# Transposing unscaled probabilities in TensorE's transposing mode, with the row sums applied behind the values

## The chip, the cores and the metric

One core of one Trainium2 chip runs the whole kernel. The metric is the device time of one execution in microseconds (us); the kernel before has a median of 924.71 us over three runs. Everything is f32 at the inputs and outputs. The engines are called TensorE (PE, and PEld for its weight loads), VectorE (DVE), ScalarE (ACT), GpSimd (POOL) and SyncE (SP, which issues most of the transfers).

## The reference

An attention with 8 batches, 8 heads, 512 local and 32 global positions of width 64 feeds a two-layer network:

```python
s_g = scale * np.matmul(q_g, k_all.transpose(0, 1, 3, 2))
out_g = np.matmul(sm(s_g), v_all)
s_ll = scale * np.matmul(q_l, k_l.transpose(0, 1, 3, 2))
mask = np.abs(pos[:, None] - pos[None, :]) <= window      # window = 32
s_ll = np.where(mask, s_ll, -1000000000.0)
s_lg = scale * np.matmul(q_l, k_g.transpose(0, 1, 3, 2))
a_l = sm(np.concatenate([s_lg, s_ll], axis=-1))
out_l = np.matmul(a_l, np.concatenate([v_g, v_l], axis=2))
# all heads side by side: x is 4352 x 512
h = x @ w_in                                                # 512 -> 2048
g = np.maximum(h, 0.0) + np.log1p(np.exp(-np.abs(h)))
out = g @ w_out                                             # 2048 -> 512
```

`sm` subtracts the row's maximum, takes the exponential and divides by the row's sum plus 1e-9.

## The kernel before

The kernel works batch by batch. The network's part is the bulk: for each batch, 16 steps `h` and `g` (first and second half of a 512-long contraction into one PSUM bank of 128x512), an activation chain on ACT, VectorE and POOL, and steps `o` that accumulate four output banks. Both use x, the weights and g as pairs of a rounded value (`hi`) and a remainder (`lo`), so each product is three matmuls. The raw f32 weights have to be taken apart into these pairs first, one tile of 128x512 at a time: `W` (ACT), `b`, `B`, `c` or `C` (the `wbits` instruction on VectorE or on ACT, then one on VectorE) and `N` or `n` (the pair on ACT and POOL, or on ACT and VectorE). All 32 tiles are done in the opening.

The attention of batches 1 to 7 works on transposed scores (`s_ps`, `v_ps`, `mt`, `zt`, `rb`). The first batch has a path of its own, in ten steps: eight local ones (four pairs of heads `m`, halves `a` of two 128-query chunks each) and two global ones. Each has seven stages, written `U<step><stage>`:

- 0, `scores0`: the mask and the scores of 4 x 128 queries by 224 keys in PSUM (`s`), the maxima and the exponentials (`e`, in SBUF) with their sums (VectorE, ACT);
- 1, `invert0`: 1/sum on VectorE;
- 2, `diag0`: POOL multiplies the 128x128 identity by 1/sum, once per score block (`diag`, 128x512);
- 3, `turn0`: plain f32 matmuls of `e` with `diag` give the scaled and transposed probabilities (`t`, one PSUM tile of two banks that all steps share);
- 4, `evict0`: two copies to SBUF (`p_..gh`, `p_..gl`; form `F` puts both on ACT);
- 5, `values0`: the product with the values (`o`, in one of the two banks that `h` uses as well);
- 6, `split0`: ACT rounds it to `xh`, VectorE takes the remainder `xl`. For the global steps (`split0g`) ACT copies it to `yg`, which is stored.

All four `xh`, `xl` of the batch must be there before the first `h`.

The order of all this work is written out by hand in three strings: `OPENING` (first batch's attention, the weights, second batch's attention and the first 16 `h`), `STEADY` (each further batch) and `LAST`. Each token issues its instructions, and `keep` and `inorder` hold each engine to that order. Helpers record each matmul at line 166 and the first batch's stages at lines 194 to 333.

Of the kernel before, what the change touches and what calls it, by code (L numbers as in the profile page):

```python
# [83 lines left out]
def moe_over_global_local_attention(  # L84
# [137 lines left out]
    def invert0(name, n):  # L222

        t = st["sums", name]
        keep("dve", nc.vector.tensor_scalar(t[:, 2, 0:n], t[:, 2, 0:n], 1e-9, None, op0=ALU.add))
        keep("dve", nc.vector.reciprocal(t[:, 0, 0:n], t[:, 2, 0:n]))

    def diag0(name, n):

        t = st.pop(("sums", name))  # L230
        d = st["diag", name] = pl.tile([P, 4, P], F32, tag="xa", name=f"diag{name}", bufs=4)
        keep("pool", nc.gpsimd.tensor_tensor(d[:, 0:n], identf.unsqueeze(1).to_broadcast([P, n, P]), t[:, 0, 0:n].unsqueeze(2).to_broadcast([P, n, P]), op=ALU.mult))
# [39 lines left out]
    def values0(m, a):  # L272
        t, vt = st.pop(("p0", m, a)), st["v0", m]
        ps = st["o0", m, a] = ps_h.tile([P, 512], F32, tag="h", name=f"o0_{m}_{a}")[:, 0:256].rearrange("p (c q) -> p c q", c=2)
        for c in range(2):
# [4 lines left out]

    def split0(m, a):
        ps = st.pop(("o0", m, a))
        if a == 0:
# [3 lines left out]
        keep("act", nc.scalar.copy(hi, ps))
        keep("dve", nc.vector.tensor_tensor(lo, ps, hi.bitcast(F32), op=ALU.subtract))
# [38 lines left out]
    def split0g(n):  # L327
        ps = st.pop(("o0g", n))
        y = pl.tile([P, 2, SG], F32, tag="yg", name=f"yg{n}", bufs=1)
        for h in range(2):  # L330
# [1 line left out]
            keep("act", nc.scalar.copy(y[r], ps[r, 0:P].rearrange("p (i h q) -> p i h q", i=2, h=2)[:, :, h]))
# [437 lines left out]
    local = (scores0, lambda m, a: invert0((m, a), 4), lambda m, a: diag0((m, a), 4), turn0, evict0, values0, split0)  # L770
    glob = (scores0g, lambda n: invert0(n, 1), lambda n: diag0(n, 1), turn0g, evict0g, values0g, split0g)
# [79 lines left out]
```

## Time and profile before

| | before |
|---|---|
| median of 3 runs | 924.71 us (923.99 to 926.71) |
| profiled execution | 925.41 us, of which the span of its instructions is 923.6 us |
| PE busy | 913.3 us, 5,242 matmuls |
| VectorE, ACT, POOL busy | 591.3, 503.9, 443.0 us |
| PE, VectorE, ACT, POOL busy between 8 and 60 us | 50.2, 37.1, 43.2, 17.2 us of 52 |
| the same between 60 and 160 us | 100.0, 87.2, 77.3, 77.4 us of 100 |
| granted TensorE clock | 0.999 |

In the rows of the profile, `t<-diag,e` is an instruction that writes tile t from tiles diag and e; `128*128 128x512` is a matmul with weights of 128x128 and an output of 128x512. In a timeline a row starts with its start and its length in us, and ends with the idle time ahead of it and what ended that. In the chain each row is one link: start, length, engine, tile, line. A row of stretches gives, for each engine, the busy us and the instructions, then the granted clock, the share of the transfer engines and GB/s.

### The profile page before, as it was taken

How to read it: one execution, taken by the hardware profiler on the slowest of the kernel's cores; microseconds unless marked ns; L12 is line 12 of the kernel's file. 1: busy time of each engine (PE TensorE's matmuls, PEld its weight loads, DVE VectorE, ACT ScalarE, POOL GpSimd, SP SyncE). 2: the span in 40 equal slices, each digit the busy share in tenths (PEclk: the TensorE clock that was granted, in tenths of full speed). 3: DMA queues.
4: the chain of work that ended last, by engine and by line, in shares of the span. 5: the costliest groups of instructions: out<-in, count | busy, mean ns of one | idle time of the engine just before them, and what ended most of it. 6: DMA issues, size and time to landing. Idle time of an engine off the chain costs nothing.

```text
span 923.6 us, 14326 instructions
## 1 busy us (share of the span) xinstructions
PE 913.3 (99%) x5242; PEld 751.2 (81%) x5242; DVE 591.3 (64%) x1324; ACT 503.9 (55%) x850; POOL 443.0 (48%) x580
## 2 busy tenths in 40 slices
PE   8999999999999999999999999999999999999997
PEld 4888788888888888888888888888888888888896
DVE  4889988477766868477766868477766868211211
ACT  5878777453554626553554636553554636644453
POOL 2358687263644546262644546272744546222221
PEclk9999999999999999999999999999999999999999
DMA  9582501302022030302021020302021010100000
GB/s 346 193 301 98 197 17 65 113 17 85 17 81 66 10 94 18 114 17 86 18 84 64 11 92 19 113 17 86 17 86 62 14 56 6 65 0 1 24 23 23
DMA packets 30694, 65.02 MB, mean 70 GB/s; under 512 B 7328, under 2 KB 7840, under 8 KB 30624
## 3 DMA queue, kind: packets, MB, share of 16 engines
q1 hardware_dynamic: 29888, 63.78, 20.5%
q8 instruction: 41, 0.67, 0.3%
q10 hardware_dynamic: 736, 0.33, 0.2%
q14 instruction: 29, 0.24, 0.1%
HBM read 54.66 MB, written 9.44 MB: 69 GB/s over the span
## 4 chain that ended last, share of the span: by engine, by line
PE 83%; DVE 7%; issue 4%; POOL 3%; ACT 3%; DMA 0%; ACTq 0%; SPq 0%; DVEq 0%; POOLq 0%
PE o L166 36%; PE h L166 33%; PE s_ps L166 6%; PE v_ps L166 4%; DVE zt L412 2%; PE t L166 1%; DVE zr L472 1%; DVE zt L460 1%; PE s L166 1%; POOL s L445 1%; DVE e L680 1%; POOL gl L684 1%; DVE rb L474 1%; ACT s L450 1%; POOL s L446 1%
## 5 line engine op out<-in xcount | busy, mean ns | idle before, releaser
L166 PE MATMUL o<-wo,gh 128*128 128x512 f32 x1088 | 340.0, 394 | 0.0
L166 PE MATMUL h<-xh,wi 128*128 128x512 f32 (+1 forms) x1152 | 339.6, 378 | 0.0
L684 POOL TENSOR_TENSOR gl<-e,gh 128x512 fp32r<-128x512 f32 x136 | 176.4, 1297 | 290.8 <-ACT gh L683 202.4
L680 DVE SCALAR_TENSOR_TENSOR e<-h,e 128x512 f32<-128x512 f32 x136 | 92.6, 681 | 250.1 <-ACT e L679 244.7
L166 PEld LDWEIGHTS h<-xh,wi 128*128 128x128 f32 x1152 | 212.0, 188 | 41.7 <-issue 1.4
L166 PEld LDWEIGHTS o<-wo,gh 128*128 128x128 f32 x1088 | 200.7, 188 | 46.6 <-issue 7.2
L166 PE MATMUL h<-xl,wi 128*128 128x512 f32 (+1 forms) x576 | 217.3, 377 | 0.0
L166 PE MATMUL o<-wo,gl 128*128 128x512 f32 x544 | 211.7, 389 | 0.0
L677 ACT ACTIVATE e<-h 128x512 f32<-128x512 f32 x136 | 80.5, 592 | 212.3 <-PE h L166 207.4
L683 ACT CAST gh<-e 128x512 fp32r<-128x512 f32 x136 | 84.4, 620 | 132.6 <-DVE e L680 132.6
L166 PEld LDWEIGHTS h<-xl,wi 128*128 128x128 f32 x576 | 108.4, 188 | 20.1
L166 PEld LDWEIGHTS o<-wo,gl 128*128 128x128 f32 x544 | 102.1, 188 | 21.6
L679 ACT ACTIVATE e<-e,one 128x512 f32<-128x512 f32 x136 | 98.6, 725 | 4.4
L445 POOL TENSOR_TENSOR s<-s,mb 128x640 f32<-128x640 f32 x56 | 88.0, 1571 | 22.7 <-DVE mb L434 21.7
L678 ACT ACTIVATE e<-e 128x512 f32<-128x512 f32 x136 | 85.9, 632 | 4.3
L450 ACT ACTIVATE s<-s 128x1024 f32<-128x1024 f32 x56 | 58.6, 1058 | 14.7 <-POOL s L446 14.7
L460 DVE TRANSPOSE_TENSOR_REDUCE zt<-s 128x32 f32<-128x1024 f32 x56 | 65.8, 1212 | 0.5 <-ACT s L450 0.5
L166 PEld LDWEIGHTS s_ps<-raw 64*128 64x128 f32 x672 | 49.6, 186 | 10.6 <-issue 9.7
L166 PE MATMUL s_ps<-raw 64*128 64x160 f32 (+1 forms) x672 | 57.3, 315 | 0.0
L446 POOL TENSOR_TENSOR s<-s,mb 128x384 f32<-128x384 f32 x56 | 56.9, 1015 | 0.0
L395 DVE TRANSPOSE_TENSOR_REDUCE mt<-s 128x32 f32<-128x1024 f32 x48 | 56.7, 1219 | 0.0
L166 PE MATMUL v_ps<-s,v 128*64 128x160 f32 (+3 forms) x784 | 53.8, 291 | 1.1 <-DVE e L680 1.1
(154 smaller groups left out, 799.9 us busy)
## 6 DMA issues: line engine op xcount, KB each, us to landing
raw<-in_qk SPq DMA_DIRECT2D x56, 368.0 KB, 3.6
v<-in_v SPq DMA_DIRECT2D x28, 384.0 KB, 3.1
wiraw<-in_w_in SPq DMA_DIRECT2D x16, 512.0 KB, 8.1
woraw<-in_w_out SPq DMA_DIRECT2D x16, 512.0 KB, 7.0
out<-ot SPq DMA_DIRECT2D x32, 256.0 KB, 2.1
v<-in_v SPq DMA_DIRECT2D x4, 512.0 KB, 9.8
raw<-in_qk SPq DMA_DIRECT2D x4, 416.0 KB, 7.2
raw<-in_qk SPq DMA_DIRECT2D x4, 352.0 KB, 4.0
```

Of the source, the lines that this page charges most:

```text
L166: order["pe"] = after(nc.tensor.matmul(*a, **k), "pe").ins
L395: inorder(nc.vector.tensor_reduce(windows(mt, 16 * p, 32, 2, 16), st["s", m, p].rearrange("p h (b k) -> p h b k", k=32), axis=AX.X, op=ALU ...
L445: inorder(engine.tensor_tensor(sw, sw, pairs(mb, QW, 0, 192, 160), op=ALU.subtract))
L446: inorder(engine.tensor_tensor(s[:, :, 160:352], s[:, :, 160:352], mb[:, :, 64:256], op=ALU.subtract))
L450: inorder(nc.scalar.activation(s, s, AF.Exp, scale=0.125))
L460: inorder(nc.vector.tensor_reduce(windows(zt, 16 * p, 32, 2, 16), st["s", m, p].rearrange("p h (b k) -> p h b k", k=32), axis=AX.X, op=ALU ...
L677: inorder(nc.scalar.activation(e, ph, AF.Abs))
L678: inorder(nc.scalar.activation(e, e, AF.Exp, scale=-1.0))
L679: inorder(nc.scalar.activation(e, e, AF.Ln, bias=one))
L680: inorder(nc.vector.scalar_tensor_tensor(e, ph, 0.0, e, op0=ALU.max, op1=ALU.add))
L683: inorder(nc.scalar.copy(gh, e))
L684: inorder(nc.gpsimd.tensor_tensor(gl, e, gh.bitcast(F32), op=ALU.subtract))
```

## The change

Stage 3 transposes `e` itself, in TensorE's transposing mode against the plain identity. 1/sum is applied to the product with the values instead. For that it has to lie along the free axis of the transposed output: in stage 1 POOL spreads it over columns (`wide`, 128x256, in a buffer that `mt` and `zt` use too), and the new stage 2 (`over0`) transposes `wide` into the second half of the values bank, from where ACT copies it to SBUF (`y`). In stage 6 VectorE multiplies values and `y`, ACT rounds the result and POOL takes the remainder (VectorE in the form `G`, used once). The global steps do the same with 128x128, and VectorE multiplies instead of ACT's copies.

```diff
-    "L10 L20 L00 L21 L01 w L11 L02 K L12 w U00 U01 W w w U02 U10 U20 b U03 U21 F04 U11 w L31 "
...
+    "L10 L00 L20 w L01 w L11 L02 l40 L30 w L12 w L21 L31 w w L22 l42 W W K b U00 U10 w "
...
-    def diag0(name, n):
-
-        t = st.pop(("sums", name))
-        d = st["diag", name] = pl.tile([P, 4, P], F32, tag="xa", name=f"diag{name}", bufs=4)
-        keep("pool", nc.gpsimd.tensor_tensor(d[:, 0:n], identf.unsqueeze(1).to_broadcast([P, n, P]), t[:, 0, 0:n].unsqueeze(2).to_broadcast([P, n, P]), op=ALU.mult))
+        w = st["wide", name] = pl.tile([P, rows_of(349 + 40)], F32, tag="mt", name=f"wide{name}", bufs=3)[:, 0:P if n == 1 else 256]
+        if n == 1:
+            keep("pool", nc.gpsimd.tensor_copy(w, t[:, 0, 0:1].to_broadcast([P, P])))
+        else:
+            for c in range(2):
+                src = windows(t[:, 0], c, 2, 2, 1).to_broadcast([P, 2, 64])
+                keep("pool", nc.gpsimd.tensor_copy(w[:, P * c:P * c + P].rearrange("p (h d) -> p h d", h=2), src))
+
+    def values_bank(key, name):
+        if key not in st:
+            st[key] = ps_h.tile([P, 512], F32, tag="h", name=name)
+        return st[key]
+
+    def over0(m, a):
+        r = st.pop(("wide", (m, a)))
+        ps = values_bank(("o0", m, a), f"o0_{m}_{a}")
+        for c in range(2):
+            mm(ps[:, 256 + P * c:256 + P * c + P], lhsT=r[:, P * c:P * c + P], rhs=identf, start=True, stop=True, is_transpose=True, skip_group_check=True)
+        y = st["y0", m, a] = pl.tile([P, 608], F32, tag="xa", name=f"y0_{m}_{a}", bufs=4)
+        keep("act", nc.scalar.copy(y[:, 0:256], ps[:, 256:512]))
...
     def turn0(m, a):
...
-                mm(ps[:n, i // 2, q:q + P], lhsT=e[:, i, o:o + n], rhs=d[:, i], start=True, stop=True, skip_group_check=True)
+                mm(ps[:n, i // 2, q:q + P], lhsT=e[:, i, o:o + n], rhs=identf, start=True, stop=True, is_transpose=True, skip_group_check=True)
...
-    def split0(m, a):
+    def split0(m, a, engine=nc.gpsimd):
...
-        keep("act", nc.scalar.copy(hi, ps))
-        keep("dve", nc.vector.tensor_tensor(lo, ps, hi.bitcast(F32), op=ALU.subtract))
+        y = st.pop(("y0", m, a))[:, 0:256]
+        keep("dve", nc.vector.tensor_tensor(y, ps[:, 0:256], y, op=ALU.mult))
+        keep("act", nc.scalar.copy(hi, y))
+        keep("pool" if engine is nc.gpsimd else "dve", engine.tensor_tensor(lo, y, hi.bitcast(F32), op=ALU.subtract))
```

The new opening has the same steps in another order, with some of them on other engines: `wbits` is on VectorE 31 times and on ACT once (before 23 and 9), `N` stands 27 times and `n` 5 times (before 26 and 6), one subtraction of the maxima (`Q51`) goes from POOL to VectorE, and one `split0` has the form `G`. The strings for the other batches are the same.

Three places of the order follow. TensorE, from the second step's scores (`s_0_1`) on, before (`raw` holds queries and keys):

```order
L166 MATMUL s_0_1_179<-raw_0_1_120 128x224 x4
L166 LDWEIGHTS ident
L166 MATMUL s_1_0_194<-mask_76,ident 128x448
L166 LDWEIGHTS ident
L166 MATMUL s_1_0_194<-mask_76,ident 128x448
L166 MATMUL s_1_0_194<-raw_1_0_112 128x224 x4
L166 MATMUL t_0_0_212<-diag(0, 0)_177,e_0_0_162 128x128
L166 MATMUL t_0_0_212<-diag(0, 0)_177,e_0_0_162 96x128
```

and now:

```order
L166 MATMUL s_0_1_193<-raw_0_1_120 128x224 x4
L166 MATMUL t_0_0_215<-identf,e_0_0_185 128x128
L166 MATMUL t_0_0_215<-identf,e_0_0_185 96x128
L166 MATMUL t_0_0_215<-identf,e_0_0_185 128x128
L166 MATMUL t_0_0_215<-identf,e_0_0_185 96x128
```

The first turn stands ahead of the third step's scores instead of behind them, and needs `e` alone. Further on in the same queue the spread sums of two steps stand behind the turn of step (1,0), ahead of the scores of (2,1):

```order
L166 MATMUL t_1_0_307<-identf,e_1_0_235 128x128
L166 MATMUL t_1_0_307<-identf,e_1_0_235 96x128
L166 MATMUL o_0_1_329<-identf,wide(0, 1)_245 128x128 x2
L166 MATMUL o_0_0_248<-identf,wide(0, 0)_212 128x128 x2
L166 LDWEIGHTS ident
L166 MATMUL s_2_1_343<-mask_76,ident 128x448
```

Step (0,1) takes its values bank here, several steps ahead of its product with the values. On ACT the first steps read before (`L219` are the exponentials, `L622` is `W`):

```order
L219 ACTIVATE e_0_0_162,sums_0_163<-s_0_0_155,sums_0_163 128x224 x4
L622 ACTIVATE wiraw_122<-wiraw_122 128x512
L219 ACTIVATE e_0_1_186,sums_1_187<-s_0_1_179,sums_1_187 128x224 x4
L219 ACTIVATE e_1_0_201,sums_0_202<-s_1_0_194,sums_0_202 128x224 x4
L266 COPY p_0_0gh<-t_0_0_212 128x512
L268 COPY p_0_0gl<-t_0_0_212 96x512
```

and now, where two `W` go ahead of the exponentials and the first copies stand one step earlier:

```order
L649 ACTIVATE wiraw_118<-wiraw_118 128x512
L649 ACTIVATE wiraw_122<-wiraw_122 128x512
L219 ACTIVATE e_0_0_185,sums_0_186<-s_0_0_178,sums_0_186 128x224 x4
L219 ACTIVATE e_0_1_200,sums_1_201<-s_0_1_193,sums_1_201 128x224 x4
L287 COPY p_0_0gh<-t_0_0_215 128x512
L289 COPY p_0_0gl<-t_0_0_215 96x512
```

More of the change, by code (lines that the diff above doesn't have):

```diff
@@ L226, in invert0, with over0g @@
         keep("dve", nc.vector.reciprocal(t[:, 0, 0:n], t[:, 2, 0:n]))
-    def diag0(name, n):
-        t = st.pop(("sums", name))
-        d = st["diag", name] = pl.tile([P, 4, P], F32, tag="xa", name=f"diag{name}", bufs=4)
-        keep("pool", nc.gpsimd.tensor_tensor(d[:, 0:n], identf.unsqueeze(1).to_broadcast([P, n, P]), t[:, 0, 0:n].unsqueeze(2).to_broadcast([P, n, P]), op=ALU.mult))
+        w = st["wide", name] = pl.tile([P, rows_of(349 + 40)], F32, tag="mt", name=f"wide{name}", bufs=3)[:, 0:P if n == 1 else 256]
[16 more added lines that the diff above has]
+        keep("act", nc.scalar.copy(y[:, 0:256], ps[:, 256:512]))
+    def over0g(n):
+        r = st.pop(("wide", n))
+        ps = values_bank(("o0g", n), f"o0g{n}")
+        mm(ps[:, P:2 * P], lhsT=r, rhs=identf, start=True, stop=True, is_transpose=True, skip_group_check=True)
+        y = st["y0g", n] = pl.tile([P, 608], F32, tag="xa", name=f"y0g{n}", bufs=4)
+        keep("act", nc.scalar.copy(y[:, 0:P], ps[:, P:2 * P]))
     def preload0(m, a):
@@ L255, in turn0 @@
         st.pop("wbank", None)
-        e, d = st.pop(("e0", m, a)), st.pop(("diag", (m, a)))
+        e = st.pop(("e0", m, a))
         ps = st["t0", m, a] = ps_a.tile([P, 2, 512], F32, tag="a", name=f"t0_{m}_{a}")
@@ L273, in values0 @@
         t, vt = st.pop(("p0", m, a)), st["v0", m]
-        ps = st["o0", m, a] = ps_h.tile([P, 512], F32, tag="h", name=f"o0_{m}_{a}")[:, 0:256].rearrange("p (c q) -> p c q", c=2)
+        ps = values_bank(("o0", m, a), f"o0_{m}_{a}")[:, 0:256].rearrange("p (c q) -> p c q", c=2)
         for c in range(2):
@@ L302, in turn0g @@
         st.pop("wbank", None)
-        e, d = st.pop(("e0g", n)), st.pop(("diag", n))
+        e = st.pop(("e0g", n))
         ps = st["t0g", n] = ps_a.tile([P, 2, 512], F32, tag="a", name=f"t0g{n}")
         for c in range(4):
-            mm(ps[:, 0, P * c:P * c + P], lhsT=e[:, P * c:P * c + P], rhs=d[:, 0], start=True, stop=True, skip_group_check=True)
-        mm(ps[0:SG, 1, 0:P], lhsT=e[:, SL:S], rhs=d[:, 0], start=True, stop=True, skip_group_check=True)
+            mm(ps[:, 0, P * c:P * c + P], lhsT=e[:, P * c:P * c + P], rhs=identf, start=True, stop=True, is_transpose=True, skip_group_check=True)
+        mm(ps[0:SG, 1, 0:P], lhsT=e[:, SL:S], rhs=identf, start=True, stop=True, is_transpose=True, skip_group_check=True)
     def evict0g(n, both=False):
@@ L319, in values0g @@
         t = st.pop(("p0g", n))
-        ps = st["o0g", n] = ps_h.tile([P, 512], F32, tag="h", name=f"o0g{n}")
+        ps = values_bank(("o0g", n), f"o0g{n}")
         for i, m in enumerate((2 * n, 2 * n + 1)):
@@ L328, in split0g @@
         ps = st.pop(("o0g", n))
+        w0 = st.pop(("y0g", n))
         y = pl.tile([P, 2, SG], F32, tag="yg", name=f"yg{n}", bufs=1)
@@ L331, in split0g @@
             r = slice(64 * h, 64 * h + 64)
-            keep("act", nc.scalar.copy(y[r], ps[r, 0:P].rearrange("p (i h q) -> p i h q", i=2, h=2)[:, :, h]))
+            o, w = (t[r, 0:P].rearrange("p (i h q) -> p i h q", i=2, h=2)[:, :, h] for t in (ps, w0))
+            keep("dve", nc.vector.tensor_tensor(y[r], o, w, op=ALU.mult))
         nc.scalar.dma_start(out=xg_dram[2 * n:2 * n + 2, :, 0:SG].rearrange("j p q -> p j q"), in_=y)
@@ L542, in step_of @@
             steps[m][0][p](*steps[m][1])
+        elif kind == "G":
+            split0(*steps[m][1], nc.vector)
         elif kind == "M":
@@ L768, in weight_halves @@
             loads(wk[1] + AHEAD)
-    local = (scores0, lambda m, a: invert0((m, a), 4), lambda m, a: diag0((m, a), 4), turn0, evict0, values0, split0)
-    glob = (scores0g, lambda n: invert0(n, 1), lambda n: diag0(n, 1), turn0g, evict0g, values0g, split0g)
+    local = (scores0, lambda m, a: invert0((m, a), 4), over0, turn0, evict0, values0, split0)
+    glob = (scores0g, lambda n: invert0(n, 1), over0g, turn0g, evict0g, values0g, split0g)
     steps = [(local, (m, a)) for m in range(M0) for a in range(2)]
```

2 lines of the change are left out of this document (1 added, 1 removed), and 22 rows, old and new, of the table OPENING.

## The prediction

> **What bounds the kernel now.** I read the share of each engine first, then the chain that ended last, then the busy time in stretches, and last the opening in order of time.
>
> ```profile
> PE 913.3 (99%) x5242; PEld 751.2 (81%) x5242; DVE 591.3 (64%) x1324; ACT 503.9 (55%) x850; POOL 443.0 (48%) x580
> PE 83%; DVE 7%; issue 4%; POOL 3%; ACT 3%; DMA 0%; ACTq 0%; SPq 0%; DVEq 0%; POOLq 0%
> ```
>
> TensorE is busy for 913.3 of 923.6 us. A busy PE is modelled, so the share alone proves little; the stretches and the pace of its groups have to say where it really waits.
>
> ```profile
> core 0: us, PE busy (x) PEld busy (x) DVE busy (x) ACT busy (x) POOL busy (x), PEclk, DMA share, GB/s
> 10.00:20.00 10.00, 9.23 (x69) 6.44 (x68) 5.52 (x14) 8.16 (x31) 3.08 (x3) 1.00 1.04 404
> 20.00:30.00 10.00, 9.29 (x89) 7.45 (x89) 6.88 (x17) 9.16 (x26) 1.04 (x1) 1.00 1.03 397
> 8.00:60.00 52.00, 50.17 (x432) 40.37 (x433) 37.11 (x79) 43.19 (x124) 17.22 (x19) 1.00 0.74 269
> 60.00:160.00 100.00, 100.00 (x548) 80.86 (x548) 87.22 (x185) 77.28 (x128) 77.35 (x86) 1.00 0.35 122
> ```
>
> Nearly all of PE's gaps lie between 10 and 30 us, with ACT at 8.2 to 9.2 of 10. Behind 60 us PE has none, and VectorE is the next engine (87 of 100). The change lies in the part before about 66 us; the steady part is the same text. So the question is how much earlier the same dense stream of `h` and `o` starts. In the chain by time (start, length, engine, tile, instructions):
>
> ```profile
> 21.41 0.44 PE o L166 x4
> 22.77 1.96 PE t L166 x16
> 38.34 1.96 PE t L166 x16
> 43.46 1.42 PE t0g L166 x10
> 58.79 2.97 PE h L166 x12
> 72.69 2.72 PE o L166 x12
> 192.69 2.73 PE h L166 x12
> ```
>
> From 21.4 us every link is PE work, up to the last row's. A `turn0` (8 calls, 16 instructions) takes 1.96 us, a `turn0g` (5 calls, 10 instructions) 1.42 us, and the first `h` starts at 58.7 us.
>
> **The change, part by part.**
>
> *Transposes.* Today 8 x 1.96 + 2 x 1.42 = 18.5 us of PE, 0.245 us a call: two load-and-multiply pairs of 0.122 us. The built program holds a transposing call as one pair: 5,242 - 148 + 92 = 5,186 matmuls. No row shows what a transposing pair costs. Bounds, from the timeline of PE:
>
> ```profile
> 37.51 0.39 PE L166 MATMUL o<-p_0gl,v 96*64 96x128 f32 x4
> 37.73 0.39 PE L166 MATMUL o<-p_0gh,v 128*64 128x128 f32 x4
> 37.95 0.39 PE L166 MATMUL o<-p_0gl,v 96*64 96x128 f32 x4
> 38.27 2.03 PE L166 MATMUL t<-diag(2, 1)_432,e 128*128 128x128 f32 x16
> 49.66 1.00 PE L166 MATMUL o0g<-p0g0gh,v 128*128 128x64 f32 x8
> 50.60 0.43 PE L166 MATMUL o0g<-p0g0gl,v 32*128 32x64 f32 x2
> ```
>
> Below: pairs with 64 weight columns start 0.22/4 = 0.055 us apart. Above: 0.245 us, the whole call of today. In between stands `o0g`: 128 weight columns and only 64 moved columns still take 0.94/8 = 0.118 us a pair, hardly less than a transpose's 0.122 with 128 moved columns. So the load of 128 f32 weights sets about 0.12 us, and a transposing call has exactly that load. I take 0.12. The 74 old calls become 8.9 us: **-9.6 us**.
>
> The Trainium skill, TensorE: Matmul & The Clock Gate, Terms, says that the transposing mode of loads and matmuls is 4 times faster for FP32. As an estimate by that page a call is 0.245/4 = 0.061 us and all 92 are 5.6 us, so PE would save 11.9 us where the sum by the rows gives 6.4; the trace of before has no such call to decide it.
>
> *The inverse sums* now pass through PE: 18 more calls x 0.12 = 2.2 us, in ten groups of their own. Between groups PE loses a little: four pairs from 37.95 would end at 38.17, the next group starts at 38.27. Ten x 0.1 = 1.0. Together **+3.2 us**. (They fill the free half of a values bank and need no wait for scores.) PE so far: **-6.4 us**.
>
> *What leaves the chain before a turn.* POOL built the scaled identity there:
>
> ```profile
> 11.14 0.68 ACT L622 ACTIVATE wiraw<-wiraw 128x512 f32<-128x512 f32 x1
> 11.30 0.17 DVE L225 TENSOR_SCALAR sums<-sums 128x4 f32<-128x4 f32 x1 [1.96 <-ACT e L219]
> 11.50 0.18 DVE L226 RECIPROCAL sums<-sums 128x4 f32<-128x4 f32 x1
> 11.76 1.04 POOL L232 TENSOR_TENSOR diag(0, 0)_177<-identf,sums 128x512 f32<-128x512 f32 x1 [8.35 <-DVE sums L226]
> 13.51 2.03 PE L166 MATMUL t<-diag(0, 0)_177,e 128*128 128x128 f32 x16
> 16.73 0.60 ACT L266 COPY p_0gh<-t 128x512 f32<-128x512 f32 x1
> 17.19 0.60 ACT L268 COPY p_0gl<-t 96x512 f32<-96x512 f32 x1
> 17.67 0.70 ACT L622 ACTIVATE wiraw<-wiraw 128x512 f32<-128x512 f32 x1
> ```
>
> From the exps (end 11.14) to a usable identity it is 1.7 us; the new turn can follow the exps at once. This pays only in the first three or four steps, where PE has gaps.
>
> *ACT.* A copy of 128x256 out of PSUM per local step (two casts of that size below take 0.66 us, so 0.33 each at most) adds 8 x 0.3 + 2 x 0.2, the global results' four copies leave (0.43 for two), and eight `wbits` of 0.67 us go to VectorE: 2.8 - 0.9 - 5.4 = -3.5 us.
>
> ```profile
> 9.44 0.45 ACT L219 ACTIVATE e<-s,sums 128x224 f32<-128x224 f32 x1 [7.41 <-DVE sums L217]
> 55.38 0.43 ACT L332 COPY yg<-o0g 64x64 f32<-64x64 f32 x2
> 23.43 0.66 ACT L287 CAST xh<-o 128x256 fp32r<-128x256 f32 x2
> 46.95 0.67 ACT L631 ACTIVATE wbitswi<-wiraw 128x512 int32<-128x512 uint8 x1
> L628 DVE TENSOR_SCALAR wbitswo<-woraw 128x512 int32<-128x512 int32 x13 | 7.3, 562 | 0.1
> L288 DVE TENSOR_TENSOR xl<-o,xh 128x256 fp32r<-128x256 f32 x8 | 3.1, 403 | 0.8 <-ACT xh L287 0.8
> L369 DVE TENSOR_TENSOR s<-s_ps,mask 128x1024 f32<-128x1024 f32 x8 | 9.7, 1212 | 1.5 <-PE s_ps L166 1.5
> ```
>
> *VectorE.* Eight `wbits` x 0.56 = 4.5; eight products of 128x256, priced as `xl` (0.40), against seven `xl` that go to POOL: +0.4; `Q51` with 1,024 columns like L369, +1.2; four small products, +0.7; one `halves` less, -0.7: **+6.1 us**, some 4 of them behind the first `h`. There VectorE goes from 87 to 91 of 100 us. That is hidden as long as PE's next `h` or `o` lies in front; where it isn't, I set **+0.2 us**. POOL loses eight `diag` of 1.04 and two small ones, and takes 18 copies of 128x128 (a small `diag`, 0.4 each, is that size) and seven `xl` (below, four in 3.33):
>
> ```profile
> 40.28 0.40 POOL L232 TENSOR_TENSOR diag<-identf,sumsg 128x128 f32<-128x128 f32 x1 [1.63 <-DVE sumsg L226]
> 158.51 3.33 POOL L597 TENSOR_TENSOR xl<-xa,xh 128x256 fp32r<-128x256 f32 x4
> ```
>
> That is -9.1 + 7.2 + 5.8 = +3.9 us on an engine that is busy for 17 of the 52 us up to 60: hidden.
>
> *Buffers.* The transposes have one PSUM tile: each turn waits for the copies of the turn before (0.48 us each on ACT: 16.73, 17.19, 17.67). The two `h` banks are held from the first of spread or values until VectorE's product. What queues behind such a wait is everything on PE, in order. I walked the new PE order with the durations above: turn (0,0) at 11.4 us (13.5 before), turn (1,0) at 19.2 behind the copies of (0,1), turn (1,1) at 28.9 behind those of (2,0), turn (3,0) at 39.8, turn (3,1) at 43.9, first `h` at 52.8. So of PE's 6.4 us about 5.9 arrive; 0.5 goes into waits for ACT's copies. ACT is the next floor: of its 43.2 us between 8 and 60 some 41 stand ahead of the last `xh`; in the new order one weight, one cast and three `wbits` fewer (-2.8) and copies (+1.9) make about 40; two weights go ahead of the first exps (9.44), which leaves 39 of the 43 us between 9.4 and 52.8.
>
> *Changes of number format.* `h` of 12 instructions takes 2.97 behind `t0g` and 2.72 elsewhere (`o` at 72.69): 0.25 us where PE goes from plain f32 to the rounded format. In the opening that happens 11 times before, 10 after: **-0.2 us**. Weights' loads and the steady tables are as before.
>
> Sum: -5.9 + 0.2 - 0.2 = -5.9 us. The profiled execution took 925.41 us (span 923.6, 1.8 around it): 919.5. The median of the runs shown is 0.7 lower: **918.8 us**.
>
> **The rivals.**
>
> 1. *Cheaper transposes.* At 0.055 us a call PE would save 12 us. ACT then is the floor: 39 us from 9.4 give 48.4 for the first `h`, some 2 more for waits, so -7.5 to -10 us: about 916. For it: nothing says that transposing loads are as slow as plain ones. Against: `o0g` at 0.118.
>
> 2. *The gain goes into waits.* Two values banks and one transposing tile on an engine that issues in order; ACT with 39 of 43 us; VectorE at 91 in 100 behind. If each of the ten steps from the second on waits 0.4 us more than in my walk, 2.3 us or less are left: 922.4 to 924.7. Against it: ACT and POOL lose work.
>
> 3. *Slower: transposing calls are paced by their whole length.* Break-even is where 92 calls and their groups cost what went: (18.5 - 1.0)/92 = 0.19 us a call.
>
> ```profile
> L166 PE MATMUL t<-diag(3, 1)_583,e 128*128 128x128 f32 x8 | 1.6, 288 | 0.0
> ```
>
> A plain transpose's instruction lasts 0.288 us from start to end and only overlap hides it. At 0.245 to 0.288, 92 calls are 22.5 to 26.5, so +5 to +9, of which the early gaps take 1: about 930. For it: an unknown mode, and ten tiny groups. Against: every other kind of call in this trace overlaps its neighbours.
>
> The Trainium skill, same page, Part 4 (PE-mode transpose), gives about 275 ns for a 128x128 transpose in one kernel's context and says that the mode doesn't count as activity for the full clock. By that figure 92 calls are an estimated 25 us, as in this rival.
>
> 4. *Slower: the clock falls.* If transposes leave PE counted as idle, the stretch from 10 to 52 us runs at the slow pace that PE shows at its start:
>
> ```profile
> 6.13 1.87 PE L166 MATMUL s<-raw 64*128 64x224 f32 x8 [1.18 <-DMA raw<-in_qk]
> 15.85 1.03 PE L166 MATMUL s<-raw 64*128 64x224 f32 x8
> ```
>
> The same eight take 1.87 at 6 us and 1.03 at 16. Were a third of the 42 us slow, that is +11: 936. Against: transposes are only 11 of these 42 us, in pieces of 1 us between matmuls. (That row of the clock reads 1.00 in every stretch quoted, so the pace of `s` would show it.)
>
> 5. *No scale is saved* (the transposing flag without effect on the time of a call, but two pairs still) is excluded by the count of 5,186.
>
> **How the numbers follow.** Forecast (-3.5 to -7.5 us, 917.2 to 921.2): 0.63. Rival 1: 0.12. Rival 2: 0.14. Rival 3: 0.09. Rival 4: 0.02. A difference of 0.3% (2.8 us) is about what a measurement of this kernel tells from none. Faster: forecast and rival 1, 0.75; same: rival 2, 0.14; slower: 0.11. The range reaches into rivals 1 and 2, 914 to 924.3, and leaves out the slower ones and the far end of the first.
>
> **What would show it.** Right: a turn of 8 instructions taking 0.95 to 1.0 us; the first `h` at 52 to 54 us; no gap on PE from there to 195 - 6 us. Rival 1 shows turns of 0.5 us; rival 3 turns of 1.9 to 2.3; rival 2 short turns, but PE waits on ACT's copies or VectorE's product before the first `h`, or `h` and `o` that wait for VectorE behind it; rival 4 an `s` of eight above 1.03 us behind 16 us. The forecast is wrong if the turns are as priced and the first `h` is not 5 to 7 us earlier, or if it is and the end is not.

## The result, and the profile after

The changed kernel takes **935.44 us** (933.91 to 937.01, 4 runs) where the kernel before takes 925.17 (923.99 to 926.71, 4 runs): a ratio of 1.0104, with an interval of 1.0091 to 1.0116. It is 1% slower; 918.8 was forecast. The profiled execution takes 936.84 us (span 935.1).

The page of the changed kernel, its shares and its chain by engine:

```profile
PE 916.9 (98%) x5186; PEld 752.2 (80%) x5186; DVE 600.1 (64%) x1338; ACT 500.4 (54%) x848; POOL 448.3 (48%) x594
PE 79%; DVE 8%; issue 4%; ACT 4%; POOL 3%; DMA 1%; SPq 0%; ACTq 0%; DVEq 0%; POOLq 0%
```

PE has 56 matmuls fewer, as forecast, and yet is busy for 3.6 us more than before. Where that is shows in the stretches of the changed kernel (columns as before; the eighth number is the granted clock):

```profile
core 0: us, PE busy (x) PEld busy (x) DVE busy (x) ACT busy (x) POOL busy (x), PEclk, DMA share, GB/s
8.00:60.00 52.00, 42.53 (x325) 32.77 (x327) 33.86 (x75) 39.11 (x119) 18.71 (x29) 0.85 0.70 261
10.00:20.00 10.00, 8.61 (x58) 5.77 (x56) 5.36 (x13) 6.92 (x28) 1.65 (x4) 0.66 1.04 402
40.00:50.00 10.00, 7.17 (x62) 5.71 (x60) 8.62 (x11) 7.26 (x21) 4.83 (x8) 1.00 0.55 193
50.00:54.00 4.00, 2.87 (x26) 2.48 (x25) 2.54 (x7) 3.91 (x10) 2.80 (x5) 0.69 0.41 111
54.00:58.00 4.00, 4.00 (x20) 3.57 (x17) 1.95 (x5) 1.87 (x4) 1.85 (x2) 0.50 0.09 33
58.00:62.00 4.00, 4.00 (x26) 3.44 (x27) 0.65 (x1) 0.00 (x0) 0.00 (x0) 0.50 0.00 0
62.00:65.00 3.00, 3.00 (x20) 2.31 (x16) 1.82 (x2) 0.27 (x1) 0.26 (x1) 0.50 0.42 126
72.00:76.00 4.00, 4.00 (x20) 3.40 (x20) 3.40 (x6) 1.30 (x2) 4.00 (x4) 0.50 1.04 409
76.00:80.00 4.00, 4.00 (x13) 3.15 (x12) 3.90 (x5) 1.41 (x3) 3.06 (x6) 0.65 0.49 172
90.00:160.00 70.00, 70.00 (x392) 56.24 (x391) 63.86 (x142) 53.03 (x86) 54.63 (x55) 1.00 0.31 107
4.00:227.17 223.17, 212.37 (x1216) 169.24 (x1214) 170.66 (x369) 146.72 (x295) 126.45 (x153) 0.94 0.38 136
```

Two things are new. PE stands idle for 9.5 of the 52 us up to 60 (1.8 before). And the clock is granted at one half from about 51.5 to 65.2 us and from 72 to 78.8 us, where the kernel before had 1.00, and earlier already from about 10.5 to 17.4 us (the 0.66 of the row from 10 to 20). Behind 90 us the stream is as dense as it was. The gaps ahead of the two later slow stretches, in the timeline of PE:

```profile
45.61 1.13 PE L166 MATMUL s0g<-raw,raw 128*128 128x256 f32 x4 [0.93 <-ACT e L219]
...
49.87 0.41 PE L166 MATMUL o<-identf,wide(3, 0)_522 128*128 128x128 f32 x2 [1.90 <-DVE y L309]
50.12 1.04 PE L166 MATMUL t<-identf,e 128*128 128x128 f32 x8
52.29 0.70 PE L166 MATMUL o<-p_0gh,v 128*64 128x128 f32 x4 [1.13 <-ACT y L246]
66.23 0.71 PE L166 MATMUL h<-xh,wi 128*128 128x512 f32 x2
70.03 1.10 PE L166 MATMUL o0g<-p0g1gh,v 128*128 128x64 f32 x8 [0.78 <-ACT y0g L253]
```

The spread sums of step (3,0) wait 1.90 us for a values bank, which VectorE's product of an earlier step holds. The values of the same step then wait 1.13 us for ACT's copy of those sums out of the same bank. The first `h` starts at 66.23, 7.5 us later than before. The chain of waits runs through VectorE and ACT for almost 11 us there, from 41.4 to 52.3 us. Its second half (start, length, link):

```profile
44.77 1.14 DVE s L394
46.00 1.25 DVE mt L397
47.25 1.36 DVE wbitswi L655
48.70 0.69 DVE wiraw L659
49.39 0.34 DVE y L309
51.87 0.38 ACT y L246
52.29 1.98 PE o L166 x16
```

A mask and a maximum of the second batch and a pair of weight bits stand in VectorE's queue ahead of the product `y` that frees the bank.

**The account.** The first group of 44 `v_ps` behind 200 us, deep in the dense part, serves as a marker: it starts at 215.74 us before and at 227.17 after, 11.43 later, which is the whole difference of the two profiled executions (936.84 - 925.41). The stretch of the kernel before from 4 us to that marker:

```profile
4.00:215.74 211.74, 208.73 (x1271) 168.25 (x1269) 161.65 (x355) 150.15 (x297) 121.18 (x139) 1.00 0.40 144
```

PE's idle time grows from 3.0 (211.74 - 208.73) to 10.8 us (223.17 - 212.37): +7.8. Its busy time grows by 3.6, though its work shrank. Experiment e12 below has the same work with the clock at 1.00 from 20 us on and gives the split: work -6.2, slow pace +9.8. Ahead of 20 us none of the three kernels runs at full pace all the time. The changed kernel and e12 each have 6.8 us at half clock there, so that part cancels between them. In the kernel before, the eight instructions of `s` take 1.86 us at 9.20 and 1.03 at 15.85, so it is at half pace until about 12 us, although its rows of the clock read 1.00; the -6.2 is therefore not a pure price of work.

### The profile page after: what moved, and what is told of

It reads as the page before. It is cut to its first block, busy times and chain, and to the rows that moved or that the text cites. A ratio compares the mean times of both kernels' runs of the same rounds, so it can differ in the third digit from the quotient of the medians.

```text
span 935.1 us, 14244 instructions
## 1 busy us (share of the span) xinstructions
PE 916.9 (98%) x5186; PEld 752.2 (80%) x5186; DVE 600.1 (64%) x1338; ACT 500.4 (54%) x848; POOL 448.3 (48%) x594
## 3 DMA queue, kind: packets, MB, share of 16 engines
HBM read 54.66 MB, written 9.44 MB: 69 GB/s over the span
## 4 chain that ended last, share of the span: by engine, by line
PE 79%; DVE 8%; issue 4%; ACT 4%; POOL 3%; DMA 1%; SPq 0%; ACTq 0%; DVEq 0%; POOLq 0%
PE o L166 35%; PE h L166 33%; PE s_ps L166 6%; PE v_ps L166 4%; DVE zt L437 2%; DVE zr L497 1%; DVE zt L485 1%; POOL s L470 1%; PE o0g L166 1%; DVE e L707 1%; DMA wiraw<-in_w_in 1%; POOL gl L711 1%; ACT e L219 1%; ACT s L475 1%; POOL s L471 1%
## 5 line engine op out<-in xcount | busy, mean ns | idle before, releaser
L166 PEld LDWEIGHTS s_ps<-raw 64*128 64x128 f32 x672 | 51.2, 192 | 10.7 <-issue 10.1
L166 PE MATMUL s_ps<-raw 64*128 64x160 f32 (+1 forms) x672 | 59.2, 322 | 0.0
```

The source lines that it names most:

```text
L166: order["pe"] = after(nc.tensor.matmul(*a, **k), "pe").ins
```

## The experiments

In order of their questions. A ratio is given where a kernel was timed in rounds; the others are one execution beside the kernel before on the same chip.

**Does a transposing call count as activity, and what does it cost?** (e4) Runs of calls alone are put ahead of the kernel before: bf16 with 512 columns (`bf`), plain f32 (two pairs a call), transposing calls, and plain f32 with 64 moved columns:

```diff
+    bf(40)
+    ff(48, P)
+    bf(16)
+    ff(96, P, is_transpose=True)
+    bf(40)
+    ff(48, 64)
+    bf(40)
```

> The kernel of before with runs of matmuls ahead of everything, back to back: 40 bf16 of 128x512, 48 plain f32 calls of 128x128, 16 bf16, 96 transposing calls of 128x128 (some 11 us), 40 bf16, 48 plain f32 calls with 64 moved columns, 40 bf16. The time is longer by these runs (about 60 us) and says nothing. Theory A: granted clock 1.00 through the transposes, the bf16 matmuls behind them start 0.22 us apart. Theory B: the clock is 0.50 from 3 to 7 us into the transposes, and the bf16 matmuls behind them start 0.43 us apart for some us.

The timeline of PE and its stretches in this kernel (columns of the stretches: us, PE busy, clock, DMA share, GB/s):

```profile
12.73 10.88 PE L166 MATMUL dummy<-identf 128*128 128x128 f32 x96
26.90 10.64 PE L166 MATMUL dummy<-identf 128*128 128x128 f32 x96
37.38 8.80 PE L166 MATMUL dummy<-warm 128*128 128x512 bf16 x40
46.01 10.83 PE L166 MATMUL dummy<-identf 128*128 128x64 f32 x96
```

```profile
20.00:30.00 10.00, 10.00 (x78) 1.00 1.03 397
30.00:40.00 10.00, 10.00 (x83) 1.00 0.34 129
```

The 96 transposing calls take 37.38 - 26.90 = 10.48 us, 0.109 a call, and the clock stays at 1.00 through them and behind them. 48 plain calls take 10.72 us, 0.223 a call. So a transposing call costs one of the two pairs of a plain one, and a dense run of them keeps the clock up. (The whole run, 983.81 us, says nothing.) Moving half as many columns saves nothing: 96 pairs still take 10.7 us.

**Is PE's time worth anything in the opening?** (e3, e5, e10, e6) In e3 the changed kernel keeps its order and takes the transposing mode off, so 92 calls are plain again (one of the five places):

```diff
-mm(ps[:n, i // 2, q:q + P], lhsT=e[:, i, o:o + n], rhs=identf, start=True, stop=True, is_transpose=True, skip_group_check=True)
+mm(ps[:n, i // 2, q:q + P], lhsT=e[:, i, o:o + n], rhs=identf, start=True, stop=True, skip_group_check=True)
```

> The changed kernel with all 92 transposing calls as plain f32 matmuls against the same identity (same results, two pairs a call, 0.245 us instead of 0.115). Theory A: the same waits on ACT and VectorE between 43 and 53 us, some of them filled by 3 to 4 us of longer turns, and the clock falls again if they still leave gaps of 2 us: 930 to 938. Theory B: the clock stays at 1.00 from 20 us on, no h or o runs at half pace, and the time is 926 to 931 although PE has 12 us more work.

**933.64 us**, a time of theory A with the clock of theory B: with some 11 us more work on PE (92 x 0.12) it is no slower than the changed kernel. Its stretches, and the row of the spread of (3,0):

```profile
40.00:50.00 10.00, 10.00 (x101) 8.46 (x98) 6.28 (x12) 7.75 (x24) 3.83 (x7) 1.00 0.19 49
50.00:60.00 10.00, 8.18 (x70) 7.32 (x71) 7.98 (x16) 7.51 (x16) 5.91 (x7) 1.00 0.58 201
4.00:223.94 219.94, 212.37 (x1308) 172.98 (x1306) 170.91 (x369) 147.45 (x295) 126.40 (x153) 0.98 0.38 138
```

```profile
53.47 0.68 PE L166 MATMUL o<-identf,wide(3, 0)_522 128*128 128x128 f32 x4 [1.82 <-DVE y L309]
```

PE has no gap between 40 and 50 us, and the clock holds through the wait of 1.82 us for the same product of VectorE. PE's busy time up to the marker is the same 212.37 as in the changed kernel, by chance: there the time went into half pace, here into longer calls. Against the kernel before, PE is busy for 3.6 us more (212.37 - 208.73) and idles 4.6 us more (219.94 - 212.37 = 7.6, from 3.0). So the waits come with the new stages and their order also where the clock stays at 1.00 (40 to 60 us). Its first `h` is at 65.41.

In e5 the kernel before keeps its order. POOL scales the exponentials in place, where it built the identity, and the turns take the transposing mode:

```diff
-        d = st["diag", name] = pl.tile([P, 4, P], F32, tag="xa", name=f"diag{name}", bufs=4)
...
+        w = e if n == 4 else e.unsqueeze(1)
+        keep("pool", nc.gpsimd.tensor_tensor(w, w, t[:, 0, 0:n].unsqueeze(2).to_broadcast([P, n, 224 if n == 4 else S]), op=ALU.mult))
...
+                mm(ps[:n, i // 2, q:q + P], lhsT=e[:, i, o:o + n], rhs=identf, start=True, stop=True, is_transpose=True, skip_group_check=True)
```

> The order of before, and its work, but POOL multiplies the exponentials themselves by 1/sum (128x896 in place, some 2.2 us instead of the scaled identity's 1.04) and the turns are in the transposing mode against the plain identity: no spread sums, no extra copy, no product. PE saves 74 x 0.13 = 9.6 us and nothing is added on ACT and VectorE. Theory A (ACT's and VectorE's queues and the PSUM tiles between them set the opening, PE's time is worth little there): no gain that comes near 9.6 us, 922 to 928, PE with gaps of 5 us or more between 24 and 60 us. Theory C (what was lost is the extra work behind the transposes, and PE's time is worth its length): 915 to 919, first h at 50 to 53 us.

**926.18 us**, ratio 1.0003 (0.9993 to 1.0012). Its stretch from 4 us to the marker:

```profile
4.00:215.31 211.31, 201.69 (x1197) 159.73 (x1195) 165.58 (x355) 149.28 (x297) 127.97 (x139) 1.00 0.40 144
```

PE is busy for 7.0 us less than before (208.73 - 201.69), and its idle time grows by 6.6 (211.31 - 201.69 = 9.6, from 3.0). The clock reads 1.00. This run alone doesn't show that the saving is worth nothing, since POOL's instruction ahead of each turn is longer as well (1.74 us on average, where the scaled identity took 1.04). The next two runs take that apart.

e10 does the scaling in two halves of 128x448; e6 leaves the division by the sums out altogether, so its time is that of a kernel that computes less:

```diff
-            keep("pool", nc.gpsimd.tensor_tensor(w, w, t[:, 0, 0:n].unsqueeze(2).to_broadcast([P, n, 224 if n == 4 else S]), op=ALU.mult))
+        for w, o, c in ((e[:, 0:2], 0, 2), (e[:, 2:4], 2, 2)) if n == 4 else ((e.unsqueeze(1), 0, 1),):
+            keep("pool", nc.gpsimd.tensor_tensor(w, w, t[:, 0, o:o + c].unsqueeze(2).to_broadcast([P, c, 224 if n == 4 else S]), op=ALU.mult))
```

> The kernel of e5 (before's order, exponentials scaled in place by POOL, then transposed unscaled) with POOL's scaling in two halves, so that the second half's wait is the only one left open. Theory A (ScalarE, VectorE and POOL set the opening, PE's saved 9.6 us do not count): between e5 (926.2) and e6 (922.7, no scaling at all): 924 to 926.5, first h at 57.3 to 58.5. Theory C (a turn's start counts, and half of POOL's time in front of each turn was what ate the gain): 921 to 923.5, first h below 56.5.

> As the run before, with the scaling left out altogether (the first batch's probabilities are not divided by their sums, so its output is not the reference's): transposing turns that wait for the exponentials alone, in the order of before. This is what PE's saving can bring at most without a new order. Theory A: 920 to 925, since ACT's queue is the same. Theory C: 913 to 916.

e10 takes **925.47 us**, ratio 0.9993 (0.9984 to 1.0003); e6 takes 922.67 beside 925.51. In e6 the transposes are cheaper and nothing is put in place of the scaling. Its marker stands at 212.70 us, and from 4 us to there PE is busy for 199.13 of 208.70 us: 9.6 less than before (208.73 - 199.13), with 6.6 more idle (208.70 - 199.13 = 9.6, from 3.0). PE waits there for ScalarE's exponentials and copies and for VectorE's `xl`. So in the order of before, of 9.6 us saved on PE some 3 arrive: ScalarE and VectorE set the pace of the opening as soon as PE is a little faster. With POOL's scaling in front of the turns (e5, e10) nothing measurable is left.

**Is it the order or the arithmetic?** (e1, e2) e1 takes the new arithmetic back into the order of before (each spread right behind its values, three other steps a little later, and the global spread sums in another buffer):

```diff
-"L10 L00 L20 w L01 w L11 L02 l40 L30 w L12 w L21 L31 w w L22 l42 W W K b U00 U10 w "
+"L10 L20 L00 L21 L01 w L11 L02 K L12 w U00 U01 W w w U10 U20 b U03 U21 F04 U11 w L31 W U30 U05 "
+"U02 U13 w F14 U31 l40 w W n c L22 U15 U12 U06 U23 U16 F24 W W w W b U40 b U25 U22 b l42 U41 U33 "
...
```

> The new arithmetic (transposing mode, spread sums, product behind the values) in the order of before: each spread follows its step's product with the values, step (1,1)'s values stand a little earlier, weights and splits where they were. Theory A (the new order makes PE wait, and the waits let the clock fall; the arithmetic itself saves): PE stays dense from about 22 us, turns of 0.92 us, first h at 52 to 56 us, granted clock 1.00 from 20 us on, time 916 to 922. Theory B (a transposing call counts as idle for the clock, whatever the order): stretches at a clock of 0.5 between 20 and 70 us, 928 or more.

e2 does the opposite: the scaled identity and plain turns of before, in the new order.

```diff
+"L10 L00 L20 w L01 w L11 L02 l40 L30 w L12 w L21 L31 w w L22 l42 W W K b U00 U10 w U01 U02 U03 "
...
     local = (scores0, lambda m, a: invert0((m, a), 4), lambda m, a: diag0((m, a), 4), turn0, evict0, values0, split0)
```

> The arithmetic of before (scaled identity from POOL, plain f32 turns, two pairs a call) in the new order, with each scaled identity right behind its inverse sum. Theory A: PE still waits for the same things early (ACT behind its two first weights until 11 us), and the time is above before's, 928 to 936; the clock may fall or not, since the plain turns fill 7 us more. Theory B: no transposing call, so the clock stays at 1.00 from 20 us on and the time is within 4 us of before's.

e1: **932.8 us**, ratio 1.0083 (1.0066 to 1.01). e2: **954.5**. Two waits of each, by the timeline of PE, e1 first:

```profile
58.64 0.44 PE L163 MATMUL o<-p_0gh,v 128*64 128x128 f32 x4 [1.77 <-DVE yg L354]
81.69 0.70 PE L163 MATMUL h<-xh,wi 128*128 128x512 f32 x2 [2.59 <-DVE yg L354]
```

```profile
14.63 3.78 PE L163 MATMUL t<-diag(0, 0)_212,e 128*128 128x128 f32 x16 [3.39 <-POOL diag(0, 0)_212 L229]
40.35 3.78 PE L163 MATMUL t<-diag(2, 0)_365,e 128*128 128x128 f32 x16 [4.37 <-POOL diag(2, 0)_365 L229]
```

The new arithmetic loses in either order. In the order of before, the values of a step and an `h` wait for VectorE's products `yg`, which hold a values bank and did not exist before. The new order suits only the new arithmetic: with a turn that has to wait for POOL it loses 29 us. Nor is it a gain: e1 is some 3 us faster than the changed kernel (932.8 against 935.44), so the new order can account for about that much of the loss, and the rest comes in either order. (e1 has neither the time of its theory A nor the clock of its theory B: two of its four executions had a mean clock of 0.998 and 0.999, as before, and took 933.02 and 932.57.)

**What makes the clock fall?** (e7, e11, e12) e7 and e11 put bf16 matmuls with an unused result into the gaps of the changed kernel. e7 puts them (8 and 5) into the tile of the second half of the global scores:

```diff
-"... F74 U56 W U90 U81 U36 U72 L32 U83 F84 U75 U65 N b W "
+"... F74 U56 W U90 f8 U81 U36 U72 L32 U83 f5 F84 U75 U65 N b W "
```

> The changed kernel with 13 bf16 matmuls of 128x448 (0.2 us each) into an unused part of the second global step's scores: eight behind these scores, where PE waits for 1.9 us from 48 us on, five behind the last local turn, where it waits for 1.1. All waits stay. Theory A: the clock stays at 1.00 from 20 to 66 us, values, global values and scores between 52 and 65 run at full pace, first h at 60 to 61 us instead of 66, time 926 to 931. If the low clock has another cause than the idle time: 935 to 937.

**934.27 us**, and no answer on the price: the filler itself waited 3.55 us for the global exponentials that read this tile. The clock was at 0.69 and 0.89 in the two stretches from 50 to 58 us and at 1.00 from there to 65. e11 puts nine into the tile that the next turn takes:

```diff
-"... W U90 U81 U36 U72 L32 U83 "
+"... W U90 U81 U36 f9 U72 L32 U83 "
+            t = st["pre"] = ps_a.tile([P, 2, 512], F32, tag="a", name=f"pre{m}")
+            for _ in range(m):
+                mm(t[:, 0, 0:448], lhsT=ident, rhs=mask[:, 0, 0:448], start=True, stop=True, skip_group_check=True)
```

> The changed kernel, with nine more bf16 matmuls of 448 columns, with an unused result, ahead of the spread sums of local step (3,0) in the PSUM tile that the next turn takes; nothing new has to be waited for but the copies out of that tile, which are done by then. They add about 2 us of PE work where PE waited 1.9 us for VectorE's product. Theory A (the halved clock, not the waits themselves, makes most of the 10 us): granted clock 0.9 or more in 50 to 65 us, first h at 60 to 62, 928 to 932; 925 to 928 if the second low stretch at 72 to 79 us goes too. Theory D (the clock is only a companion, the work then waits for ScalarE and VectorE instead): clock near 1.0 but first h still at 65 to 66, 934 to 936. If the clock is still 0.5 there, the fill says nothing on the price.

**930.07 us**, in the range of the theory that the clock makes most of it. The timeline of PE and a stretch of it:

```profile
47.90 1.86 PE L163 MATMUL pre<-mask,ident 128*128 128x448 bf16 x9
49.83 0.41 PE L163 MATMUL o<-identf,wide(3, 0)_522 128*128 128x128 f32 x2
52.25 0.44 PE L163 MATMUL o<-p_0gh,v 128*64 128x128 f32 x4 [1.13 <-ACT y L243]
60.61 0.72 PE L163 MATMUL h<-xh,wi 128*128 128x512 f32 x2
```

```profile
54.00:58.00 4.00, 4.00 (x44) 3.55 (x43) 2.20 (x4) 1.72 (x4) 1.77 (x2) 1.00 0.07 25
```

This is the cleanest pair of the study. The spread of (3,0) and the values of (3,0) start within 0.05 us of where they start in the changed kernel (49.87 and 52.29). Only the 1.9 us ahead of the spread were filled. The clock holds there, and the first `h` comes at 60.61 and not at 66.23: 5.6 us earlier, with more work and the same wait of 1.13 us. A short stretch at half clock from about 67.6 to 71 us is left.

e12 moves one step of e11, so that a copy doesn't stand behind six ScalarE items at 64 us:

```diff
-"... F94 M4 W W N W P41 D50 N U92 h g E41 U95 "
+"... F94 M4 U92 W W N W P41 D50 N h g E41 U95 "
```

> The kernel of e11 with one step moved: the spread of the second global step (U92), with its copy on ScalarE, goes ahead of the weight work (W W N W) that stood in front of it, so that the copy no longer stands behind six ScalarE items. Theory A (this wait of 0.79 us at 64 us and the half clock at 67 to 71 us that follows it are one cause): gap below 0.2, granted clock 1.00 from 60 to 80 us, 927 to 928.5. Theory E (the half clock at 67 comes from something else, the DMA traffic of that stretch for one): gap gone, clock still 0.5 for some 3.4 us, 929 to 930.5.

**929.62 us**: the clock as theory A had it, the time as theory E had it. Its stretch from 4 us to the marker, and two rows of PE's timeline:

```profile
4.00:219.87 215.87, 204.41 (x1224) 162.56 (x1223) 170.53 (x369) 146.61 (x295) 126.31 (x153) 0.98 0.39 141
```

```profile
60.59 0.30 PE L163 MATMUL o0g<-identf,wide 128*128 128x128 f32 x1 [0.99 <-DVE yg L354]
69.69 0.74 PE L163 MATMUL h<-xh,wi 128*128 128x512 f32 x2 [1.12 <-DVE e L709]
```

The clock is now 1.00 from 20 us on, the other wait (0.79 at 64 us) has gone, and the time hardly moves: one wait of 0.99 us for VectorE's `yg` and one of 1.12 for its work on `h` have come in its place. Less the filler (204.41 - 1.86) PE's work is 202.55 us, 6.2 less than before. The changed kernel needed 212.37 for the same: 9.8 us of half pace. That fits the two later slow stretches: of their 20.4 us PE idles for 0.8 (51.5 to 52.3), and half of the 19.6 it is busy is 9.8. Against the kernel before, e12's PE idles 8.5 us more (215.87 - 204.41 = 11.5, from 3.0) and is busy 4.3 us less, filler and all: the difference is the 4.1 us by which its marker comes later.

**Can the waits be ordered away?** (e8, e9, e13) e8 puts the two weights behind the first exponentials and one pair of weight bits (`b`) behind the product that it stood ahead of; e9 also puts the values of (3,0) ahead of its spread. The second line is e8's, the third e9's:

```diff
-"... l42 W W K b U00 U10 w ... U73 U52 b N F74 U56 W U90 U81 U36 U72 L32 U83 F84 U75 U65 "
+"... l42 K U00 U10 W W b w ... U73 U52 N F74 U56 b W U90 U81 U36 U72 L32 U83 F84 U75 U65 "
+"... l42 K U00 U10 W W b w ... U73 U52 N F74 U56 b W U90 U81 U36 L32 U83 F84 U75 U72 U65 "
```

> The changed kernel with two places of its order mended: the two first weights' instructions (ACT and VectorE) go behind the exponentials of the first two steps, and one pair of weight bits on VectorE goes behind the product of step (2,1) that PE waits for at 48 us. Theory A: the first turn starts at 10.5 us instead of 12.1, the gap at 48 us shrinks from 1.9 to under 0.5 us, and if the clock then holds the time is 924 to 930; if it doesn't, 932 to 935.

> The kernel of e8 (two weights behind the first exps, a pair of weight bits earlier), with one step more moved: the values of local step (3,0) (U75) go ahead of its spread sums (U72), so that they no longer wait for ScalarE's copy out of the same bank. Theory A (single waits of 1 to 3 us in the sparse stretch at 45 to 54 us cost themselves and then the clock): the 3.0 us wait of e8 at 48 to 51 us goes, the granted clock in 50 to 65 us stays above 0.9, first h at 57 to 60, time 925 to 930. Theory B (the order has too little ready work there whatever stands first, the wait passes to the next step): another wait of 2 us or more within 8 us, clock again near 0.5 for some 7 us, 933 to 937.

e8: **935.7 us**. e9: **932.27**. A row of PE's timeline in each, e8 first:

```profile
51.12 0.70 PE L163 MATMUL o<-p_0gh,v 128*64 128x128 f32 x4 [3.00 <-ACT y L243]
```

```profile
50.86 1.10 PE L163 MATMUL o0g<-p0g0gh,v 128*128 128x64 f32 x8 [0.79 <-DVE y L306]
```

In e8 the wait of 1.90 us has gone and the next one has grown from 1.13 to 3.00. In e9 that has gone too, and the next values wait 0.79 for their bank; the clock is at 0.50 from about 53 to 60 us all the same, so e9 is nearer to the second theory.

e13 adds to e9 the move of e12 and six fillers ahead of the global values:

```diff
-"... F84 U75 U72 U65 N b W ... F94 M4 W W N W P41 D50 N U92 h "
+"... F84 U75 U72 f6 U65 N b W ... F94 M4 U92 W W N W P41 D50 N h "
```

> The kernel of e9 (weights behind the first exps, values of (3,0) ahead of its spread) with the step of e12 moved too, and six bf16 matmuls of 448 columns with an unused result ahead of the values of the first global step, where e9 waited 0.8 us and its clock halved. Theory A (waits and the clock they cost made the whole loss): clock 1.00 from 16 us on, first h at 57 to 59, 923.5 to 926, so about the kernel before or up to 0.3% faster; PE's forecast 6 us do not come, since ScalarE and VectorE set the opening. Theory F (the new arithmetic itself costs elsewhere, with VectorE's added work behind the first h): clock 1.00 but 928 or more.

**929.87 us**, ratio 1.0038 (1.0023 to 1.0052), the time of the second theory, but without its condition: the clock was 0.81 and 0.76 in the two stretches from 50 to 58 us. The filler's tile was still being copied out, so the filler waited itself:

```profile
52.66 2.40 PE L163 MATMUL pre<-mask,ident 128*128 128x448 bf16 x6 [2.34 <-ACT p_1gl L286]
```

No kernel of the study that computes the same result beats the one before by more than its measurement is uncertain; e10 is the nearest.

## Why the prediction was wrong, point by point

**The price of a call was right.** A turn of eight was forecast at 0.95 to 1.0 us; a typical one takes 18.90 - 17.98 = 0.92, 0.115 a call (0.109 by itself in e4) where 0.12 was taken. Rivals 1 and 3, cheaper or dearer calls, are out. In e6, where the calls get cheaper and nothing is added on PE, it is busy 9.6 us less, as forecast; in the changed kernel its work shrank by 6.2 us, early slow pace included, where -6.4 stood. Fewer moved columns save nothing (e4), so the load of 128 weights as what sets the price, read off the row of `o0g`, holds up. The Trainium skill's four times for FP32 (TensorE: Matmul & The Clock Gate, Terms) is two times here, and its remark in Part 4 that the transposing mode doesn't count as activity is not what e4 shows.

**ScalarE, GpSimd and VectorE.** ScalarE: -3.5 forecast, 503.9 to 500.4 measured. GpSimd: +3.9 forecast, +5.3 measured. VectorE: +6.1 forecast, +8.8 measured (591.3 to 600.1). Behind the opening "91 of 100" was right (63.86 of 70) and it is hidden there.

**The step that failed is the walk of PE's order**: "of PE's 6.4 us about 5.9 arrive; 0.5 goes into waits for ACT's copies". PE waits 7.8 us more, not 0.5, and the sum has no term for a lower clock, where 9.8 us of half pace came. The turns are short and PE waits on ACT's copies and VectorE's product ahead of the first `h`: the sign that the prediction gave for rival 2. The walk went off in three places:

- "Two weights go ahead of the first exps" was counted as ScalarE work alone. They need weights that are still on their way. The timeline of ScalarE in the changed kernel:

```profile
11.00 0.65 ACT L649 ACTIVATE wiraw<-wiraw 128x512 f32<-128x512 f32 x1 [1.69 <-DMA wiraw<-in_w_in]
11.55 0.43 ACT L219 ACTIVATE e<-s,sums 128x224 f32<-128x224 f32 x1
```

  The first exponentials start at 11.55 us and not at 9.44, so the first turn starts at 12.13 where 11.4 stood. By turn (1,0) the walk was 2.8 us early (19.2 against 22.02); the slow stretch from 10.5 to 17.4 us, in which the eight instructions of `s` take 1.87 us, lies in there too. This start matters little for the end: in e8 the first turn is at 10.82 and the clock is back by 13 us, and it is no faster.

- The spread sums "need no wait for scores", which is true, but they need a values bank. The prediction says that a bank is held until VectorE's product, yet for the opening it prices only "waits for ACT's copies": that the product stands in order behind weight and mask work on VectorE has no term. It also missed that values have to wait for ScalarE's copy when spread and values share a bank. By turn (3,1) the walk was 6.2 us early (43.9 against 50.12).

- "ACT is the next floor", with 39 of 43 us, was a sum of busy times. It says that the work would fit, not that it comes in time. VectorE had no such floor for the opening at all, and it ends the longest wait behind 40 us.

**The gain was priced as if PE set the opening.** PE was dense from 30 to 60 us before, but ScalarE, VectorE and POOL were only just ahead of it. e6 shows the effect without any reordering and with nothing added: 9.6 us less work, 6.6 us more idle time. Rival 2, gain into waits, named the mechanism; its range, 922.4 to 924.7 us, ended where the whole gain is gone. The waits took all 6.2 us and 1.6 more, and the halved clock came on top.

**The clock.** Rival 4 gave 936 us and a chance of 0.02. Its number is that of the result by chance, for its reason doesn't hold: a run of transposes keeps the clock up (e4). The waits that rival 2 brings thin out PE's work, and the thinning halves the clock. That they belong together was not seen: the two rivals were priced apart. e11 and e12, one execution each, show its size: 5.4 to 5.8 us of the 10.3 between the medians (935.44 - 930.07 and - 929.62), with the filler's own 1.9 us in the way. The changed kernel's own executions point the same way: 936.84 and 937.01 us at a mean clock of 0.985 and 0.984, 934.04 and 933.91 at 0.988. The remaining 3.6 to 4 us against the kernel before stand, in e12, with the clock at 1.00 from 20 us on, and are waits that outweigh the saving (8.5 us more idle time, 4.3 less work). A low clock doesn't always cost time: e10 takes 925.1 to 925.75 us in five executions with a mean clock of 0.994 and 925.27 to 926.19 in the five with 0.998 to 1.00.

**Buffers and formats.** The term of 0.2 us for format changes lies below anything that these runs resolve.

What stays open: the waits are not settled one by one. Taking one away (e8, e12) brought the next, and no order was found in which the new arithmetic wins. Nor was it settled which gap trips the clock: the profiled e5 has gaps of up to 1.35 us and keeps 1.00, and e3 keeps it through one of 1.82 in dense work, while e9 loses it behind gaps of 0.91 and 0.79. One kernel's executions also differ (0.994 to 1.00 in e10), so a single trace doesn't say what an order does to the clock every time.

## What to carry to other kernels

Before pricing a saving on the busiest engine, look at how far ahead of it the others are. In this opening ScalarE was busy for 43 and VectorE for 37 of 52 us, and of 9.6 us saved on PE some 3 arrived (e6). A new stage that holds a shared bank until another engine's product belongs into that engine's queue in the walk, with everything that stands ahead of it there. And price waits on TensorE together with the clock: in this kernel gaps of one and two microseconds in sparse work were followed by a halved clock, and holding the clock up won 5.4 to 5.8 us of the 10.3 that were lost.

## What the runs showed of the hardware

**The clock can fall on gaps well below 3 us, and stays down in steps.** In the changed kernel no gap between 40 and 60 us is longer than 1.90 us, and the clock falls at about 51.5; with that gap filled (e11) it doesn't. The slow stretches, worked out from the granted clock of the rows (a row of 4 us at 0.69 holds 2.5 us at 0.50): 10.5 to 17.4 is 6.8 us, 51.5 to 65.2 is 13.6 us, 72.0 to 78.8 is 6.8 us, and in e11 67.6 to 71.0 is 3.4 us: twice, four times, twice and once 3.4. The Trainium skill (TensorE: Matmul & The Clock Gate, Part 1) gives a window of about 3.4 us, and the lengths agree with it; its advice, in the section Why this matters for your kernels, to allow no idle gaps of more than about 3 us between bursts, is not enough here. Behind 52.3 us PE is busy throughout in the two later stretches, as the rows from 54 to 65 us show for the first: a dense stream at half pace did not bring the clock back within 3.4 us.

**A VectorE instruction that starts inside a GpSimd product can wait for its end.** Rows of VectorE and one of GpSimd in the timeline of the changed kernel:

```profile
43.55 0.41 DVE L655 TENSOR_SCALAR wbitswi<-wiraw 128x512 int32<-128x512 int32 x1
47.17 1.42 DVE L655 TENSOR_SCALAR wbitswi<-wiraw 128x512 int32<-128x512 int32 x1
47.02 1.29 POOL L665 TENSOR_TENSOR wo<-woraw,wo 128x512 fp32r<-128x512 f32 x1 [3.40 <-ACT wo L664]
```

The same instruction takes 0.41 us at 43.55, with almost no GpSimd work beside it, and 1.42 us when it starts 0.15 us into a GpSimd product that ends at 48.31; it ends 0.28 behind that. This 1.0 us lies on the chain of the 1.90 us gap. The Trainium skill (SBUF — State Buffer, Who interferes with whom) has the two engines share a pair of ports as an exclusive lock, held by whichever starts first; this row agrees. Other rows agree: of the eight scalings of 128x4 maxima (L217), five run beside no GpSimd product and take 0.17 us. Three start inside one, at 21.64, 35.17 and 42.58; they take 0.22, 0.92 and 1.06 us and each ends 0.02 behind that product (21.84, 36.07, 43.62). Copies on GpSimd don't show it: a pair of weight bits that starts at 51.44, 0.10 into two of them, takes 0.47. No run here took the overlap away, so it is a reading of the rows and not a tested cause.
